# Attention, channel mix and MLP on one core: a pause in score making at block ends, an earlier place for turned loads, a z tile doubled on chip

## The chip, the core and the metric

The kernel runs on one core of a Trainium2 chip. The metric is device time in microseconds. Three runs of the kernel before took 2532.66 to 2536.51 us, median 2535.36 us. The engines are TensorE (PE in the profile; its weight loads are PEld), VectorE (DVE), ScalarE (ACT), GpSimd (POOL) and SyncE (SP), which here only issues transfers.

## What is computed

Three stages follow each other, all in float32. Batch 4, sequence S = 3072, width 256.

```python
scores = (1 / S) * z @ z.T                  # z: 4 x 3072 x 64
x = u * (maximum(scores, 0) ** 2 @ v)       # attention without softmax
xk, xr = mixes of x with x one position back, by mu_k and mu_r
k = maximum(xk @ w_k, 0) ** 2               # 256 -> 1024
x = sigmoid(xr @ w_r) * (k @ w_v)           # 1024 -> 256
out = maximum(x @ w_in, 0) ** 2 @ w_out     # 256 -> 2048 -> 256
```

`u`, `v`, `z` arrive in float32. The weights arrive in float64 and are turned into float32 on the chip by bit operations (`convert`, eight VectorE steps for each piece and two more for a split).

## The kernel before, in words

**Precision.** Every operand of a matmul is split into a high and a low part (`hi` is the operand rounded to the matmul's type, `lo` the rest), and a product takes three matmuls: high by high, high by low of the other side, low by high.

**Tiling of the attention.** Scores are symmetric, so the kernel makes them transposed: a chunk is 128 key positions by a block of T = 512 query positions. A batch has NB = 6 blocks, a block NJ = 24 chunks in NG = 6 groups of G = 4; four batches give 24 blocks and 576 steps. Step s of the main loop (L519) takes chunk s: `attend` (L394) multiplies the chunk with the matching rows of v and adds to two accumulators `d` = 0, 1, each in two halves of 64 rows which two matmuls fill side by side. In a step with j = s mod 24 the order on TensorE differs at a block's ends: steps 0 and 22 do the accumulator 0 alone, steps 1 and 23 catch up on accumulator 1. So step 0 has three pairs of matmuls, steps 1 and 23 nine, step 22 three, and the others six. Within step 0 and 1, all three terms of an accumulator follow each other, the low part of the chunk last.

**Making a chunk.** `scores(s)` (L357) makes a chunk in one of two ways. For a group g at or right of the block's diagonal (g >= ib, ib being the block's number in its batch) TensorE computes two chunks at once into score banks (L371, four banks), ScalarE applies ReLU (L354) and squares (L375), ScalarE or VectorE casts the high part (L380 or L378), VectorE turns the chunk for later use (`turn`, L332, when g > ib) and subtracts the low part (L385). For g < ib the chunk was already computed in its transposed form: it was turned, stored to memory, and is loaded again by `load_turned_scores` (L341) in four quarters q into one of three buffers `mixed`; then it takes only a cast (L363) and a subtraction (L364). The subtraction of a chunk is not issued with it: `finish` (L387) holds it back and issues it when the next chunk is made. In the last block of a batch, the diagonal group comes first.

**Lead.** Chunks are made ahead of their use. The loop at L537 makes chunks up to s + 4 at first, and up to s + 7 later: the lead is 4 up to step 71, 5 up to 95, 6 up to 119 and 7 from step 120. Chunk tiles (`ahi`, `alo`) have eight buffers.

**End of a block.** `gate` (L406) copies the accumulators out. For d = 0, ScalarE copies both halves (L410 `x` and L413 `rest`); for d = 1 it copies one, and VectorE adds the other (L417). Then VectorE adds the halves of d = 0 (L415), multiplies both by the turned u (L424, twice), and SP stores them (L426). The accumulators have one buffer each, so the next block's first matmul waits for L413.

**Order of the work.** The scheduler is off (`manual_schedule`): each engine runs its instructions in the order in which the program issues them, and SP issues transfers in that order as well. The list `todo` holds what a step issues before its own matmuls, in the order of registration (`at_step`): z, v, u loads and their preparation, the weight conversions, and the quarters of turned loads. z tiles are loaded with two copies of the 64 rows (four transfers of 32 partitions each), transposed by VectorE (L267), cast by ScalarE (L274) and subtracted by VectorE (L276). `load_v` (L278) and `prep_v` (L290) do the same for v, through three buffers `raw` that the weight pieces use too.

The two later stages (`channel_mix`, `mlp`) take the rest of the time; the change does not touch them.

Of the kernel before, what the change touches and what calls it, by code (L numbers as in the profile page):

```python
# [7 lines left out]
F32 = mybir.dt.float32  # L8
# [3 lines left out]
ALU = mybir.AluOpType  # L12
# [3 lines left out]
P = 128  # L16
Q = 32
T = 512
# [3 lines left out]
def tile_relu2_attention__rwkv_channel_mix__relu2_mlp(  # L22
# [18 lines left out]
    nc = tc.nc  # L41
# [200 lines left out]
    def attention():  # L242
        with ExitStack() as st:
# [11 lines left out]
                engine.dma_start(out=t[p:p + Q].rearrange("q (k r) -> q k r", r=Q),  # L255
                                 in_=src.rearrange("(q k) r -> q k r" if g in apart else "(k q) r -> q k r", q=Q))

            def load_z(b, g, engines=(nc.sync,) * R):
                z_raw[b, g] = t = io.tile([P, T], F32, tag="zn", name="zn")
                for k, e in enumerate(engines):  # L260
                    d = k * Q % DQ
                    load_turned(t, k * Q, z[b, g * T:(g + 1) * T, d:d + Q], g, e)

            def prep_z(b, g, stage):
                if stage == 0:
                    zT[b, g] = io.tile([P, T], F32, tag="zT", name="zT", bufs=1)
                    nc.vector.transpose(zT[b, g], z_raw.pop((b, g)))  # L267
                    return
                t = zT[b, g]
                if stage == 1:  # L270
                    if g % 2 == 0:
                        zz[b] = zp.tile([P, G, T], F32R, tag="zz", name="zz", bufs=NG // 2)
                    zhi[b, g], zlo[b, g] = (zz[b][:, i, :] for i in (g % 2 * 2, g % 2 * 2 + 1))
# [83 lines left out]
            def scores(s):  # L357
                n, b, ib, g, c = chunk(s)
                if g < ib:
                    a = ready[n, g][:, :, c].rearrange("y p c k -> y c p k")  # L360
                    hi, lo = at[s] = parts(*pools["hidden"])
                    hi_v, lo_v = (t.rearrange("y (c p k) -> y c p k", c=G, k=Q) for t in (hi, lo))
                    nc.scalar.copy(hi_v, a)  # L363
                    finish(lambda: nc.vector.tensor_tensor(out=lo_v, in0=a, in1=hi_v, op=ALU.subtract))  # L364
                    return
                ps = ()
                if c % 2 == 0:
                    ps = [ps_s.tile([P, T], F32, tag="w", name="sps") for _ in HALVES]
                    for k in range(3):
                        for i, rows in enumerate(HALVES):  # L370
                            nc.tensor.matmul(ps[i], lhsT=(zlo, zhi, zhi)[k][b, g][rows, (c + i) * P:(c + i + 1) * P],  # L371
                                             rhs=(zhi, zlo, zhi)[k][b, ib][rows], start=k == 0, stop=k == 2)
                    rel[s] = relu(ps[0])
                a = rel.pop(s)
                nc.scalar.activation(out=a, in_=a, func=AF.Square)  # L375
                hi, lo = at[s] = parts(*pools["hidden"])
                if (g == ib and ib < 3) or (ib < 2 and c == 3) or (ib == 0 and c == 1 and g % 2):
                    nc.vector.tensor_copy(hi, a)  # L378
                else:
                    nc.scalar.copy(hi, a)  # L380
# [53 lines left out]
                todo.setdefault(s, []).append((f, a))  # L434

            n_steps = NBLK * NJ
            for b in range(1, B):
                end = b * NB * NJ
                for g in range(NG):
                    s = end + NJ * (g // 2 - 3) + 6 + 9 * (g % 2)  # L440
                    at_step(s, load_z, b, g)
                    for k in range(3):
                        at_step(s + 7 + 2 * k, prep_z, b, g, k)
                    s = end - NJ + G * ((g + 1) % NG) + 5
                    at_step(s - 8, load_v, b, g)
                    for h in range(2):
                        for lo in range(2):
                            at_step(s + 2 * h + lo, prep_v, b, g, h, lo)
# [4 lines left out]
            for g in range(1, NG):  # L453
                if g > 1:
                    at_step(max(-FIRST, G * g - 15), load_z, 0, g)
                at_step(max(-FIRST, G * g - 12), load_v, 0, g)
                for k in range(3 if g > 1 else 0):
                    at_step(max(1 - FIRST, G * g - 11) + k, prep_z, 0, g, k)
                for h in range(2):
                    for lo in range(2):  # L460
                        at_step(G * g - 5 + 2 * h + lo, prep_v, 0, g, h, lo)
# [3 lines left out]
                    at_step(s + 2 + 9 * d, load_u, n, d)  # L465
                    at_step(s + 10 + 9 * d, prep_u, n, d)

            freed, taken, EARLY = [], 0, 30
            for n in range(NBLK - 1):
                b, ib = divmod(n, NB)  # L470
                for g in range(ib):
                    need, stored = n * NJ + (g + ib // (NB - 1)) * G - LEAD, (b * NB + g) * NJ + ib * G + G - 1 - FIRST
                    s = max(need - EARLY, stored + 1, freed[-3] if len(freed) > 2 else 0, taken)
                    d = max(1, min(3, (need - 3 - s) // 4))
                    for q in range(R):
                        at_step(s + q * d, load_turned_scores, n, g, q)
                    taken = s + 4 * d
                    assert taken <= need - 2
                    freed.append(need + G + 1)
            for g in range(NB - 1):  # L480
                for q in range(R):
                    at_step((NBLK - 1) * NJ + G * g - (15 if g < 2 else 10) + q, load_turned_scores, NBLK - 1, g, q)
            conversions = []
            for w, sb in ((w_k, wk), (w_v, wv), (w_r, wr)):
                for src, cs, fs in pieces(w.bitcast(U32), 2):
# [4 lines left out]
                                lambda: nc.vector.tensor_tensor(out=lo, in0=t, in1=hi, op=ALU.subtract)]  # L490
                    conversions.append((src, keep, 2))
            later = LEAD - FIRST
            free = [t for t in range(NJ, n_steps - NJ) if chunk(t + later)[3] < chunk(t + later)[2] < NB - 1]
            total = sum(8 + rests for _, _, rests in conversions)
            k0 = 0
            for i, (src, done, rests) in enumerate(conversions):
                steps = [free[(k0 + k) * len(free) // total] for k in range(8 + rests)]
                k0 += len(steps)
# [3 lines left out]
            assert total <= len(free)  # L502

            s = n_steps - NJ
            for n in range(2):
                at_step(s - 6 + 12 * n, load_x, n)
# [5 lines left out]
            for wh, m in enumerate((mu_k, mu_r)):  # L512
                nc.sync.dma_start(out=mu[:, wh, :], in_=m.rearrange("(c p) -> p c", p=P))
            for g in range(2):
                for k in range(3):
                    prep_z(0, g, k)
            nc.vector.tensor_scalar(out=om, in0=mu, scalar1=-1.0, scalar2=1.0, op0=ALU.mult, op1=ALU.add)
            made = 0
            for s in range(-FIRST, n_steps + 1):  # L519
                for f, a in todo.pop(s, ()):  # L520
                    f(*a)
                if made == n_steps:
                    finish()
                j = s % NJ if 0 <= s < n_steps else None
                if j in (1, NJ - 1):
                    attend(s, 0, range(3))
                    if j > 1:
                        gate(s // NJ, 0)
                    attend(s - 1, 1, range(3))
# [404 lines left out]
```

## Time and profile before

| | us |
|---|---|
| median of three runs | 2535.36 |
| the profiled execution | 2534.24 |
| its span, first to last instruction | 2532.4 |
| TensorE busy | 2491.6 (98%) |
| VectorE busy | 1967.3 (78%) |
| ScalarE busy | 1725.6 (68%) |
| mean granted clock of TensorE | 0.995 |

Matmuls are pipelined, so a busy TensorE may still run below its peak: at half the clock it is busy as well. The clock has two levels, 1.2 and 2.4 GHz, and the granted clock of a stretch is given as a share of the higher one. The attention fills the time up to about 955 us; there TensorE's chain shows L403 (attend) and L371 (scores). Idle time of an engine that is not on the chain costs nothing by itself.

### The profile page before, as it was taken

How to read it: one execution, taken by the hardware profiler on the slowest of the kernel's cores; microseconds unless marked ns; L12 is line 12 of the kernel's file. 1: busy time of each engine (PE TensorE's matmuls, PEld its weight loads, DVE VectorE, ACT ScalarE, POOL GpSimd, SP SyncE). 2: the span in 40 equal slices, each digit the busy share in tenths (PEclk: the TensorE clock that was granted, in tenths of full speed). 3: DMA queues.
4: the chain of work that ended last, by engine and by line, in shares of the span. 5: the costliest groups of instructions: out<-in, count | busy, mean ns of one | idle time of the engine just before them, and what ended most of it. 6: DMA issues, size and time to landing. Idle time of an engine off the chain costs nothing.

```text
span 2532.4 us, 39521 instructions
## 1 busy us (share of the span) xinstructions
PE 2491.6 (98%) x14832; PEld 2047.4 (81%) x14832; DVE 1967.3 (78%) x3318; ACT 1725.6 (68%) x3015; POOL 0.2 (0%) x4
## 2 busy tenths in 40 slices
PE   7999999999999999999999999999999999999998
PEld 6877788788778878888888888788888888888887
DVE  7786977787777776888888777877777777777776
ACT  7877987788778765555655566666666666666665
POOL 0000000000000000000000000000000000000000
PEclk9999999999999999999999999999999999999999
DMA  8687677676876861222212112100110011100100
GB/s 208 161 207 180 176 199 180 183 206 161 210 191 171 196 159 55 79 84 67 88 59 87 61 48 67 31 20 17 34 34 17 18 34 34 26 25 18 34 17 17
DMA packets 322096, 244.31 MB, mean 96 GB/s; under 512 B 213104, under 2 KB 231536, under 8 KB 321904
## 3 DMA queue, kind: packets, MB, share of 16 engines
q1 hardware_dynamic: 319792, 241.39, 36.2%
q8 instruction: 116, 1.90, 0.3%
q10 hardware_dynamic: 2112, 0.39, 0.1%
q14 instruction: 76, 0.62, 0.1%
HBM read 136.86 MB, written 104.86 MB: 95 GB/s over the span
## 4 chain that ended last, share of the span: by engine, by line
PE 87%; ACT 5%; DVE 3%; DMA 2%; issue 1%; SPq 1%; DVEq 0%; ACTq 0%
PE v L403 25%; PE ups L722 16%; PE ups L208 13%; PE v L738 6%; PE v L739 6%; PE v L740 6%; PE sps L371 4%; PE v L230 3%; PE v L231 3%; PE v L234 3%; ACT a L375 1%; ACT a L354 1%; DMA mixed<-turned 1%; SPq L255 1%; ACT s L762 0%
## 5 line engine op out<-in xcount | busy, mean ns | idle before, releaser
L403 PE MATMUL v<-ahi,vhl 64*128 64x512 f32 x4608 | 646.1, 391 | 14.3 <-ACT rest L413 14.3
L403 PEld LDWEIGHTS v<-ahi,vhl 64*128 64x128 f32 x4608 | 440.2, 186 | 113.2 <-ACT rest L413 20.2
L759 ACT ACTIVATE s<-s 128x512 f32<-128x512 f32 x288 | 181.2, 629 | 333.5 <-DVE s L754 333.4
L403 PE MATMUL v<-alo,vhl 64*128 64x512 f32 x2304 | 381.0, 390 | 7.0 <-DVE alo L385 5.9
L722 PE MATMUL ups<-d,win 128*128 128x512 f32 x1152 | 323.6, 389 | 0.0
L738 PE MATMUL v<-hhi,wout 128*128 128x512 f32 x768 | 299.3, 390 | 0.9 <-ACT hhi L767 0.6
L740 PE MATMUL v<-hlo,wout 128*128 128x512 f32 x768 | 299.2, 390 | 0.5 <-DVE hlo L773 0.5
L739 PE MATMUL v<-hhi,wout 128*128 128x512 f32 x768 | 298.8, 389 | 0.0
L208 PE MATMUL ups<-mixed,wk 128*128 128x512 f32 x1152 | 291.8, 389 | 0.0
L773 DVE TENSOR_TENSOR hlo<-s,hhi 128x512 fp32r<-128x512 f32 x384 | 264.5, 689 | 21.8 <-ACT hhi L767 8.9
L160 ACT ACTIVATE a<-ups 128x512 f32<-128x512 f32 x192 | 114.9, 599 | 238.4 <-PE ups L208 231.6
L403 PEld LDWEIGHTS v<-alo,vhl 64*128 64x128 f32 x2304 | 222.3, 186 | 56.4 <-DVE alo L385 10.3
L208 PEld LDWEIGHTS ups<-mixed,wk 128*128 128x128 f32 x1152 | 216.2, 188 | 44.9
L722 PEld LDWEIGHTS ups<-d,win 128*128 128x128 f32 x1152 | 216.3, 188 | 44.8
L722 PE MATMUL ups<-b,win 128*128 128x512 f32 x864 | 242.9, 389 | 0.0
L385 DVE TENSOR_TENSOR alo<-a,ahi 128x512 fp32r<-128x512 f32 x336 | 220.6, 660 | 26.5 <-ACT ahi L380 24.3
L762 ACT ACTIVATE s<-s 128x512 f32<-128x512 f32 x384 | 231.2, 627 | 6.1
L332 DVE STREAM_TRANSPOSE turn<-a 128x512 f32<-128x512 f32 x240 | 169.4, 706 | 71.6 <-ACT a L375 71.6
L354 ACT ACTIVATE a<-sps 128x512 f32<-128x512 f32 x336 | 198.6, 591 | 31.4 <-PE sps L371 30.9
L375 ACT ACTIVATE a<-a 128x512 f32<-128x512 f32 x336 | 212.5, 633 | 10.1
L363 ACT CAST ahi<-mixed 128x512 fp32r<-128x512 f32 x220 | 126.5, 619 | 104.6 <-PE v L403 42.5
L722 PEld LDWEIGHTS ups<-b,win 128*128 128x128 f32 x864 | 162.0, 188 | 34.2 <-DVE sv L754 0.8
(103 smaller groups left out, 3672.1 us busy)
## 6 DMA issues: line engine op xcount, KB each, us to landing
mixed<-turned SPq DMA_DIRECT2D x220, 256.0 KB, 4.6
turned<-turn SPq DMA_DIRECT2D x36, 1024.0 KB, 5.2
turned<-turn SPq DMA_DIRECT2D x96, 256.0 KB, 4.0
u<-in_u_dram SPq DMA_DIRECT2D x192, 64.0 KB, 3.8
x2d<-xo SPq DMA_DIRECT2D x48, 256.0 KB, 2.2
x<-x2d SPq DMA_DIRECT2D x12, 1024.0 KB, 4.8
out_dram<-y SPq DMA_DIRECT2D x94, 128.0 KB, 2.8
x<-xT SPq DMA_DIRECT2D x20, 513.0 KB, 4.0
```

The lines of the kernel that those rows point to most:

```text
L208: nc.tensor.matmul(ps, lhsT=lhs(h, c, f), rhs=rhs[:, m, c, :], start=k == 0, stop=k == 3 * ND - 1)
L354: nc.scalar.activation(out=a, in_=ps, func=AF.Relu, scale=1.0 / S)
L375: nc.scalar.activation(out=a, in_=a, func=AF.Square)
L385: finish(lambda: nc.vector.tensor_tensor(out=lo, in0=a, in1=hi, op=ALU.subtract))
L403: nc.tensor.matmul(acc[n, d][i], lhsT=vt[rows, k % 2, c, ds_], rhs=at[s][k // 2][rows], start=first and k == 0, stop=last and k == 2)
L722: nc.tensor.matmul(ps, lhsT=win[q][:, h, r, w], rhs=x(y), start=first and m == 0, stop=m == 2, skip_group_check=not first)
L738: nc.tensor.matmul(acc[p, b][d], lhsT=w[:, 0, c, ds_], rhs=hi, start=first, stop=False)
L739: nc.tensor.matmul(acc[p, b][d], lhsT=w[:, 1, c, ds_], rhs=hi, start=False, stop=False)
L740: nc.tensor.matmul(acc[p, b][d], lhsT=w[:, 0, c, ds_], rhs=lo, start=False, stop=last)
L759: nc.scalar.activation(out=tmp[g, c], in_=banks[g, 0] if c == "11" else tmp[g, c], func=AF.Relu, scale=HS)
L762: nc.scalar.activation(out=tmp[g, c], in_=tmp[g, c], func=AF.Square)
L773: nc.vector.tensor_tensor(out=lo, in0=tmp.pop((g, c)), in1=hi, op=ALU.subtract)
```

## The change

The loop makes no chunk in steps j = 21 and 22 of a block; what is missing is made in step 23, after the gates. The turned loads are registered first, so that in a step they are issued ahead of z, u and v, and the release of their buffers is planned one step earlier (`need + G` for `need + G + 1`). From batch 1 on, a z tile is loaded once (64 rows) and transposed in 64 partitions, and a transfer from on-chip memory to on-chip memory makes the second copy; the cast follows four steps after the transposition instead of two. The third and later z tiles of batch 0 are prepared two steps later. The weight conversions are spread over the batches, so that none reaches from one batch into the next. The loads of mu and `om` move from the start to steps 48 and 72. The condition of the cast's engine becomes wider: VectorE casts all chunks of the diagonal group and every fourth chunk of a group.

```diff
-            def load_z(b, g, engines=(nc.sync,) * R):
+            def load_z(b, g, engines=None):
                 z_raw[b, g] = t = io.tile([P, T], F32, tag="zn", name="zn")
-                for k, e in enumerate(engines):
+                for k, e in enumerate(engines or (nc.sync,) * (R if b == 0 else R // 2)):
                     d = k * Q % DQ
                     load_turned(t, k * Q, z[b, g * T:(g + 1) * T, d:d + Q], g, e)
 
             def prep_z(b, g, stage):
                 if stage == 0:
-                    zT[b, g] = io.tile([P, T], F32, tag="zT", name="zT", bufs=1)
-                    nc.vector.transpose(zT[b, g], z_raw.pop((b, g)))
+                    rows = slice(0, P if b == 0 else DQ)
+                    zT[b, g] = t = io.tile([P, T], F32, tag="zT", name="zT", bufs=1)
+                    nc.vector.transpose(t[rows], z_raw.pop((b, g))[rows])
+                    if b > 0:
+                        nc.sync.dma_start(out=t[DQ:P], in_=t[rows])
                     return
...
-                if (g == ib and ib < 3) or (ib < 2 and c == 3) or (ib == 0 and c == 1 and g % 2):
+                if g == ib or c == 3 or (ib == 0 and c == 1 and g % 2):
                     nc.vector.tensor_copy(hi, a)
...
+            freed, taken, EARLY = [], 0, 30
+            for n in range(NBLK - 1):
+                b, ib = divmod(n, NB)
+                for g in range(ib):
+                    need, stored = n * NJ + (g + ib // (NB - 1)) * G - LEAD, (b * NB + g) * NJ + ib * G + G - 1 - FIRST
+                    s = max(need - EARLY, stored + 1, freed[-3] if len(freed) > 2 else 0, taken)
+                    d = min(3, (need - 3 - s) // 4) or 0.5
+                    for q in range(R):
+                        at_step(s + int(q * d), load_turned_scores, n, g, q)
+                    taken = s + int(4 * d)
+                    assert taken <= need - 2
+                    freed.append(need + G)
...
             for b in range(1, B):
...
                     at_step(s, load_z, b, g)
                     for k in range(3):
-                        at_step(s + 7 + 2 * k, prep_z, b, g, k)
+                        at_step(s + (7, 11, 13)[k], prep_z, b, g, k)
...
                 for k in range(3 if g > 1 else 0):
-                    at_step(max(1 - FIRST, G * g - 11) + k, prep_z, 0, g, k)
+                    at_step(G * g - 9 + k, prep_z, 0, g, k)
...
-            freed, taken, EARLY = [], 0, 30
-            for n in range(NBLK - 1):
...
-                    d = max(1, min(3, (need - 3 - s) // 4))
-                    for q in range(R):
-                        at_step(s + q * d, load_turned_scores, n, g, q)
-                    taken = s + 4 * d
-                    assert taken <= need - 2
-                    freed.append(need + G + 1)
...
-            free = [t for t in range(NJ, n_steps - NJ) if chunk(t + later)[3] < chunk(t + later)[2] < NB - 1]
-            total = sum(8 + rests for _, _, rests in conversions)
-            k0 = 0
             for i, (src, done, rests) in enumerate(conversions):
+                b = i * B // len(conversions)
+                mine = [k for k in range(len(conversions)) if k * B // len(conversions) == b]
+                free = [t for t in range(b * NB * NJ, (b + 1) * NB * NJ - NJ)
+                        if chunk(t + later)[3] < chunk(t + later)[2] < NB - 1]
+                k0, total = (i - mine[0]) * (8 + rests), len(mine) * (8 + rests)
                 steps = [free[(k0 + k) * len(free) // total] for k in range(8 + rests)]
...
+            at_step(2 * NJ, load_mu)
+            at_step(3 * NJ, make_om)
...
-                while made < min(n_steps, s + 1 + min(LEAD, FIRST + max(0, s - 2 * NJ) // NJ)):
+                ahead = 0 if j in (NJ - 3, NJ - 2) else min(LEAD, FIRST + max(0, s - 2 * NJ) // NJ)
+                while made < min(n_steps, s + 1 + ahead):
                     scores(made)
                     made += 1
```

## Rows read from the trace of the kernel before

**Rows 1.** The page: busy time, share and instructions of each engine.
```profile
PE 2491.6 (98%) x14832; PEld 2047.4 (81%) x14832; DVE 1967.3 (78%) x3318; ACT 1725.6 (68%) x3015; POOL 0.2 (0%) x4
```

**Rows 2.** Waits of TensorE, whole span: total us, times, longest us.
```profile
PE v L403 <- ACT rest L413: 14.3, 7, 3.7
...
PE sps L371 <- ACT a L354: 4.5, 5, 2.0
```

**Rows 3.** Table by stretches: length, busy us by engine, granted clock, DMA share, GB/s.
```profile
218.60:260.40 41.80, 39.08 (x312) 31.37 (x312) 30.43 (x50) 25.91 (x48) 0.00 (x0) 0.93 0.68 184
260.40:300.00 39.60, 39.58 (x348) 32.66 (x350) 35.81 (x64) 35.17 (x62) 0.00 (x0) 1.00 0.77 214
...
493.30:534.00 40.70, 40.69 (x344) 34.55 (x346) 35.99 (x64) 35.14 (x61) 0.00 (x0) 0.96 0.76 208
...
687.00:729.00 42.00, 39.41 (x312) 31.25 (x312) 29.46 (x49) 25.16 (x48) 0.00 (x0) 0.92 0.71 181
```

**Rows 4.** Timeline of TensorE at three block ends: start, us, [idle before, releaser].
```profile
218.59 1.22 PE L403 MATMUL v<-ahi,vhl 64*128 64x512 f32 x4 [3.65 <-ACT rest L413]
...
260.42 0.73 PE L403 MATMUL v<-ahi,vhl 64*128 64x512 f32 x4 [2.70 <-ACT rest L413]
...
493.31 0.73 PE L403 MATMUL v<-ahi,vhl 64*128 64x512 f32 x4 [2.70 <-ACT rest L413]
```

**Rows 5.** The chain that ended last, one piece: start us, us, what.
```profile
72.06 2.72 PE v L403 x24
```

**Rows 6.** Timeline of SP and ScalarE, 239 to 248 us.
```profile
239.70 3.52 SPq L285 DMA_DIRECT2D raw<-in_v_dram  x4
243.27 0.59 SPq L348 DMA_DIRECT2D mixed<-turned  x1
...
246.53 1.14 ACT L363 CAST ahi<-mixed 128x512 fp32r<-128x512 f32 x2 [6.17 <-PE v L403]
```

**Rows 7.** Groups by line: the two casts; count, busy us, mean ns, idle before.
```profile
L380 ACT CAST ahi<-a 128x512 fp32r<-128x512 f32 x240 | 149.3, 622 | 7.7
...
L378 DVE CAST ahi<-a 128x512 fp32r<-128x512 f32 x96 | 40.3, 420 | 24.7 <-ACT a L375 24.1
```

**Rows 8.** Timeline of TensorE and VectorE at the first four block ends.
```profile
61.70 0.62 PE L403 MATMUL v<-ahi,vhl 64*128 64x512 f32 x4
64.38 0.68 DVE L364 TENSOR_TENSOR alo<-mixed,ahi 128x512 fp32r<-128x512 f32 x1
...
100.46 0.70 PE L403 MATMUL v<-ahi,vhl 64*128 64x512 f32 x4
103.82 1.29 DVE L364 TENSOR_TENSOR alo<-mixed,ahi 128x512 fp32r<-128x512 f32 x2
...
139.21 0.68 PE L403 MATMUL v<-ahi,vhl 64*128 64x512 f32 x4
143.34 0.67 DVE L364 TENSOR_TENSOR alo<-mixed,ahi 128x512 fp32r<-128x512 f32 x1
144.06 0.73 PE L403 MATMUL v<-alo,vhl 64*128 64x512 f32 x4 [0.72 <-DVE alo L364]
...
177.29 0.70 PE L403 MATMUL v<-ahi,vhl 64*128 64x512 f32 x4
181.48 0.67 DVE L364 TENSOR_TENSOR alo<-mixed,ahi 128x512 fp32r<-128x512 f32 x1
```

**Rows 9.** Timeline of the first block: waits of VectorE, TensorE and ScalarE.
```profile
13.40 0.71 DVE L267 STREAM_TRANSPOSE zT<-zn 128x512 f32<-128x512 f32 x1 [1.88 <-DMA zn<-in_z_dram]
15.07 0.79 PE L403 MATMUL v<-alo,vhl 64*128 64x512 f32 x2 [3.00 <-DVE alo L385]
...
38.34 0.62 ACT L274 CAST zz<-zT 128x512 fp32r<-128x512 f32 x1 [1.97 <-DVE zT L267]
```

**Rows 10.** Transfers by line: queue, count, KB each, median us from issue to landing.
```profile
mixed<-turned SPq DMA_DIRECT2D x220, 256.0 KB, 4.6
...
zn<-in_z_dram SPq DMA_DIRECT2D x94, 64.0 KB, 3.5
```

More of the change, by code (lines that the diff above doesn't have):

```diff
@@ L265, in prep_z @@
                 if stage == 0:
-                    zT[b, g] = io.tile([P, T], F32, tag="zT", name="zT", bufs=1)
-                    nc.vector.transpose(zT[b, g], z_raw.pop((b, g)))
+                    rows = slice(0, P if b == 0 else DQ)
[3 more added lines that the diff above has]
+                        nc.sync.dma_start(out=t[DQ:P], in_=t[rows])
                     return
-                t = zT[b, g]
+                t, k = zT[b, g], g % 2 * 2
                 if stage == 1:
@@ L272, in prep_z @@
                         zz[b] = zp.tile([P, G, T], F32R, tag="zz", name="zz", bufs=NG // 2)
-                    zhi[b, g], zlo[b, g] = (zz[b][:, i, :] for i in (g % 2 * 2, g % 2 * 2 + 1))
+                    zhi[b, g], zlo[b, g] = (zz[b][:, k + i, :] for i in range(2))
                     nc.scalar.copy(zhi[b, g], t)
@@ L436, in attention @@
             n_steps = NBLK * NJ
+            freed, taken, EARLY = [], 0, 30
[10 more added lines that the diff above has]
+                    freed.append(need + G)
+            for g in range(NB - 1):
+                for q in range(R):
+                    at_step((NBLK - 1) * NJ + G * g - (15 if g < 2 else 10) + q, load_turned_scores, NBLK - 1, g, q)
             for b in range(1, B):
@@ L466, in attention @@
                     at_step(s + 10 + 9 * d, prep_u, n, d)
-            freed, taken, EARLY = [], 0, 30
-            for n in range(NBLK - 1):
[L470 to L473, printed above, removed]
-                    d = max(1, min(3, (need - 3 - s) // 4))
-                    for q in range(R):
-                        at_step(s + q * d, load_turned_scores, n, g, q)
-                    taken = s + 4 * d
-                    assert taken <= need - 2
-                    freed.append(need + G + 1)
-            for g in range(NB - 1):
-                for q in range(R):
-                    at_step((NBLK - 1) * NJ + G * g - (15 if g < 2 else 10) + q, load_turned_scores, NBLK - 1, g, q)
             conversions = []
@@ L492, in attention @@
             later = LEAD - FIRST
-            free = [t for t in range(NJ, n_steps - NJ) if chunk(t + later)[3] < chunk(t + later)[2] < NB - 1]
-            total = sum(8 + rests for _, _, rests in conversions)
-            k0 = 0
             for i, (src, done, rests) in enumerate(conversions):
+                b = i * B // len(conversions)
[3 more added lines that the diff above has]
+                k0, total = (i - mine[0]) * (8 + rests), len(mine) * (8 + rests)
                 steps = [free[(k0 + k) * len(free) // total] for k in range(8 + rests)]
-                k0 += len(steps)
                 at_step(steps[0] - 10, load_raw, ("w", i), src, src.shape[1], src.shape[2])
@@ L501, in attention, with load_mu, make_om @@
                     at_step(t, f)
-            assert total <= len(free)
+                assert total <= len(free)
+            def load_mu():
+                for wh, m in enumerate((mu_k, mu_r)):
+                    nc.sync.dma_start(out=mu[:, wh, :], in_=m.rearrange("(c p) -> p c", p=P))
+            def make_om():
+                nc.vector.tensor_scalar(out=om, in0=mu, scalar1=-1.0, scalar2=1.0, op0=ALU.mult, op1=ALU.add)
+            at_step(2 * NJ, load_mu)
+            at_step(3 * NJ, make_om)
             s = n_steps - NJ
@@ L511, in attention @@
             load_v(0, 0)
-            for wh, m in enumerate((mu_k, mu_r)):
-                nc.sync.dma_start(out=mu[:, wh, :], in_=m.rearrange("(c p) -> p c", p=P))
             for g in range(2):
@@ L516, in attention @@
                     prep_z(0, g, k)
-            nc.vector.tensor_scalar(out=om, in0=mu, scalar1=-1.0, scalar2=1.0, op0=ALU.mult, op1=ALU.add)
             made = 0
```

## The prediction, made before the changed kernel ran

> **What bounds the kernel now.** I read the page's busy times first. TensorE is busy for 98% of the span [rows 1], so a change of order can only take away TensorE's pauses and its slow stretches. Next I read the waits of TensorE itself, over the whole span: 14.3 us in seven waits for the copy `rest` of L413, and 4.5 us in five waits of the score matmuls for a ReLU of L354 [rows 2]. Then the table by stretches, for the granted clock: three stretches in which the attention passes from one block to the next stand at 0.93, 0.92 and 0.96, where the block between two of them has 1.00 [rows 3]. A share below 1 is time at 1.2 GHz instead of 2.4, and each microsecond there does half a microsecond of work. So 41.8 us at 0.93 lose 0.07 x 41.8 = 2.9 us, 42.0 at 0.92 lose 3.4, 40.7 at 0.96 lose 1.6; together 7.9. Last, the timeline around the seven waits: they stand at the ends of blocks, the longest being 3.65 us, and two of 2.70 shown beside it [rows 4]. All lie in the attention; the two MLP stages are not touched.
>
> One unit is needed: 24 matmuls of 64 rows, two of which run side by side, take 2.72 us [rows 5]. So two chunk steps are 2.72, one is 1.36, and a term of one accumulator pair (two matmuls) is 0.227 us.
>
> **What takes time at the end of a block.** TensorE may only start the next block when ScalarE has copied the accumulators out (L410, L413). ScalarE has chunk work queued ahead of those copies. One source of lateness is a late turned load: SP held the load of the last quarter behind four v loads until 243.27, and ScalarE, idle for 6.17 us, began the cast at 246.53 [rows 6] (the row names TensorE, which had long been done; the load is what came last). The block's end then waited 2.70 us, until 260.42 [rows 4]. The pattern stands three times, once at the end of each of the first three batches.
>
> **The change, part by part.**
>
> *Turned scores first, no chunk in steps 21 and 22.* In steps 21 and 22 ScalarE's queue now holds no chunk ahead of the copies, and in step 23 three chunks come after them. The quarters are issued a step earlier and ahead of the v and z loads of their step. Of the 14.3 us I let all go except 1.5 at the boundary from block 4 to 5 (worked out below) and 1 at the start of each later batch: there every chunk needs ReLU and square, and the three chunks that were put off stand in front of the ReLU which frees the score banks, so TensorE waits at L371 instead. Bounds of that remainder: 0, and the 2.70 seen there. 14.3 - 1.5 - 3 = 9.8. The score waits came from the late loads: 4.5 less 0.5 at the start of the program gives 4.0. The slow stretches followed these waits; all 7.9 go. Sum so far 21.7.
>
> *More casts on VectorE.* 72 casts (18 per batch: in blocks 2 to 5 all four chunks on the diagonal from block 3 on, and the fourth chunk of each group to its right) move from 622 ns on ScalarE to 420 ns on VectorE [rows 7]. That is 45 us off ScalarE, which is late at block ends, and 30 us onto VectorE. I give it no term of its own: it is one more reason for the 9.8. Its cover is VectorE's idle time in these stretches (30.4 busy of 41.8 [rows 3]).
>
> *The price: a low part that is now late.* The low part of a chunk (L364 or L385) is issued with the chunk after it. With nothing made in steps 21 and 22, the low part of the chunk made in step 20 comes in step 23, behind the four gate operations L417, L415 and twice L424. How late that is, rows tell: at the end of block 2 TensorE has done the block at 139.21, and the first low part after the gates runs from 143.34 to 144.01. TensorE already waits for it in the kernel before, 0.72 us, until 144.06 [rows 8]; there it is the third chunk of the block. How early TensorE needs it depends on the lead. It is 7 chunks from step 120 on, and then the late one is the fourth of the new block, wanted after 0.68 + 2.04 + 1.36 + 0.91 = 4.99 us against 4.80 at which it is there: no wait. But the lead is 4 up to step 71, 5 in step 95 and 6 in step 119. With 4, the late low part belongs to the first chunk of the block, wanted 0.45 us after the block begins. I set the end of the first low part after the gates against the need [rows 8]:
> - block 0 to 1: 65.06 (64.38 + 0.68) against 61.70 + 0.45: 2.9 us
> - block 1 to 2: 104.46 (half of two in 1.29, from 103.82) against 100.46 + 0.45: 3.6
> - block 2 to 3: 144.01 against 139.21 + 0.45: 4.4, less the 0.7 that already stood there
> - block 3 to 4 (lead 5, one step of 0.68 more): 182.15 against 177.29 + 0.68 + 0.45: 3.7
> - block 4 to 5 (lead 6): there at 4.80 plus a cast of 0.42, wanted at 0.68 + 2.04 + 0.91 = 3.63: 1.5, as taken above.
>
> The first four add 13.9 us of waits. Queued behind the waiting matmul is all of TensorE's work, and nothing later gives the time back.
>
> Waits of this length may also halve the clock. Rows go both ways: after 3.65 us the stretch stands at 0.93 (2.9 us lost); after 2.70 at 260.42 it stays at 1.00; after the other 2.70, at 0.96 (1.6 lost) [rows 3, 4]. Bounds: none of four falls, 0; all fall, 4 x 2.9 = 11.6. I take 6, the two longer ones falling. The Trainium skill, TensorE: Matmul & The Clock Gate, section "What's actually happening", says that the slow clock is the default state and that activity releases it. By that rule each long wait would be paid again behind it, and the sum would be near the upper bound; the stretch at 1.00 after 2.70 us does not agree with it for every wait.
>
> *Third z tile later.* At the start VectorE stands at the transpose of the third z tile (waiting for its load, 1.88 us, until 13.40), and the first low part stands behind it; TensorE waits 3.00 us, until 15.07 [rows 9]. Moved two steps on, the first low part needs only its own cast: I take 2.5 of the 3.0 (bounds 0 and 3.0). The same for the sixth tile: ScalarE waits 1.97 us for its transpose, until 38.34 [rows 9], in a block in which TensorE waits for ScalarE's chunks: 2.0 (bounds 0 and 2.0). Sum 4.5. The two loads of `mu` and the small VectorE operation on them leave the start too; I cost that at nothing.
>
> *z doubled on chip.* In batches 1 to 3 a z tile takes two loads of 64 KB instead of four, and one copy of 128 KB from the transposed half. Loads of z land after 3.5 us, the turned quarters of 256 KB after 4.6 [rows 10]; the copy lies between or near these, and ScalarE asks for it four steps later, about 5.4 us. At nothing, since chunks lie ready ahead. What it costs when that cover is gone is the third rival.
>
> *Conversions inside a batch.* The same 90 small operations in other steps, in stretches where VectorE has room [rows 3]; at nothing, bound by one such operation of 0.7 us on either side per batch.
>
> **Sum.** 21.7 + 4.5 - 13.9 - 6 = 6.3 us gained. The profiled execution took 2534.24 us, 1.84 more than its span; by the change 2527.9. The median of the runs shown is 1.12 above it, so 2529.0.
>
> **The rivals.**
> 1. *The early low parts are not late* (something issues them ahead of the gates, or TensorE has other work there). Then the 13.9 and the 6 fall away: 26.2 gained, 2509. Against it: the wait at 144.06 is this very queue.
> 2. *They are late, but the clock holds*: 12.3 gained, 2523. For it speaks the 1.00 behind 260.42.
> 3. *Slower: SP is held, and ScalarE behind it.* A turned load in step 21 of some blocks (3 to 4, 9 to 10, 15 to 16, 21 to 22) takes over a buffer whose last low part now waits behind the gates, to 4.8 us after the block's end. Behind it in SP's queue stands the new z copy of step 22. Issued some 1.2 us later and landed after 4.6 [rows 10], it lets ScalarE cast z and the next chunk by 4.8 + 1.2 + 4.6 + 2 x 0.62 = 11.8; TensorE wants that chunk (the tenth of the block) at 0.68 + 2.04 + 7 x 1.36 = 12.2. So it decides from a landing of 5.0 us on. With 8 us TensorE would wait 3.4 in three blocks, and at 2.9 of slow clock each that is 19 lost: 12.6 slower, 2548. Against it: 4.6 is the usual landing. The Trainium skill, DMA: Bandwidth & Descriptors, section "Anatomy of one DMA", says that any semaphore wait happens on the issuing sequencer before dispatch; that is the hold described here.
> 4. *No change*: all four early waits drop the clock (11.6 instead of 6): 0.7 gained, 2534.7. This is what the clock rule cited above would make of it.
>
> **How the numbers follow.** Forecast 0.42, rival 1 0.12, rival 2 0.18, rival 3 0.12, rival 4 0.16. About 0.2%, 5 us, is what a measurement of this kernel can tell from no change: faster is below 2530.3, slower above 2540.4. The forecast's own range is 2523 to 2535, from the clock's bounds; 0.7 of it counts as faster. Faster: 0.42 x 0.7 + 0.12 + 0.18 = 0.60; slower: rival 3, 0.12; within: 0.28. The range 2512 to 2538 leaves out the far end of rivals 1 and 3.
>
> **What would show it.** In the profile after: no wait of TensorE for L413 over 1 us; new waits of TensorE for L364 or L385 of 3 to 4.5 us at the first four block ends, near 60, 100, 139 and 178 us, and none at those of later batches; granted clock under 1 in two of these four stretches and 1.00 where it was 0.92 to 0.96; the first wait for a low part at the start gone. The forecast is wrong if the early block ends show no such wait (2509), or if TensorE waits in blocks 4, 10, 16 and 22 for ScalarE while ScalarE waits for z.

## The result: 0.56% slower, and where the profile after shows it

The changed kernel took 2548.9 us (median of six runs, 2543.57 to 2551.91), before on the same chip 2534.69: a ratio of 1.0056, with a 95% interval of 1.0043 to 1.0069. The forecast was 2529 us, 6.3 gained; 14.2 were lost. The profiled execution of the changed kernel, called after below, took 2547.61 us, its span 2545.8. The lines named here have moved by up to three: the copy `rest` is now L416, a turned chunk's low part L367, a fresh chunk's L388, the attention's matmul L406, the ReLU L357, the z cast L277; the new z copy is L270.

First the page's busy times of after, against [rows 1]: VectorE has 72 instructions of the casts more, ScalarE 72 fewer and 40.5 us less work, as the change says. TensorE's share stays at 98%.

```profile
PE 2495.3 (98%) x14832; PEld 2061.4 (81%) x14832; DVE 1988.6 (78%) x3390; ACT 1685.1 (66%) x2943; POOL 0.2 (0%) x4
```

Next the waits of TensorE in after (total us, times, longest us).

```profile
PE v L406 <- DVE alo L367: 18.9, 6, 4.1
PE v L406 <- DVE alo L388: 6.8, 7, 3.9
...
PE v L406 <- ACT rest L416: 5.5, 4, 2.0
PE sps L374 <- ACT a L357: 2.5, 3, 0.8
```

Against [rows 2] the waits for `rest` went from 14.3 us to 5.5 and those of the score matmuls from 4.5 to 2.5. In their place stand 18.9 us for the low parts of turned chunks. Four of these six are the late low parts of the prediction. The timeline of after at the third of them (start, us, what, and in brackets the idle time before with its releaser) shows the queue:

```profile
151.57 0.69 DVE L420 TENSOR_TENSOR x<-v,x 128x512 f32<-128x512 f32 x1 [1.84 <-ACT x L413]
152.18 0.68 DVE L418 TENSOR_TENSOR x<-rest,x 128x512 f32<-128x512 f32 x1
152.89 1.04 DVE L427 TENSOR_TENSOR rest<-x,uT 128x512 f32<-128x512 f32 x1
153.97 1.04 DVE L427 TENSOR_TENSOR x<-x,uT 128x512 f32<-128x512 f32 x1
154.85 1.88 DVE L367 TENSOR_TENSOR alo<-mixed,ahi 128x512 fp32r<-128x512 f32 x3
155.58 0.61 PE L406 MATMUL v<-alo,vhl 64*128 64x512 f32 x2 [4.14 <-DVE alo L367]
```

The low part starts behind the four gate operations, and TensorE starts when it is done. The other three end at 67.38, 111.38 and 198.46, after 2.81, 3.40 and 3.43 us; a fifth, for a fresh chunk's low part, at 239.43 after 1.11. [rows 8] are the first places before.

The other two of the six were not in the forecast. The longer one stands at the last block of the first batch, where TensorE had its best chance to gain. Timeline of after, SP, ScalarE, VectorE and TensorE:

```profile
258.74 4.32 SPq L255 DMA_DIRECT2D u<-in_u_dram  x4
259.16 0.70 DVE L268 STREAM_TRANSPOSE zT<-zn 64x512 f32<-64x512 f32 x1 [3.49 <-DMA zn<-in_z_dram]
263.24 2.80 SPq L288 DMA_DIRECT2D raw<-in_v_dram  x4
266.14 0.54 SPq L270 DMA_DIRECT2D zT<-zT  x1
269.20 0.62 ACT L277 CAST zz<-zT 128x512 fp32r<-128x512 f32 x1 [4.10 <-DMA zT<-zT]
271.01 0.43 DVE L381 CAST ahi<-a 128x512 fp32r<-128x512 f32 x1 [6.40 <-ACT a L378]
271.35 0.69 DVE L367 TENSOR_TENSOR alo<-mixed,ahi 128x512 fp32r<-128x512 f32 x1
272.09 0.79 PE L406 MATMUL v<-alo,vhl 64*128 64x512 f32 x2 [3.54 <-DVE alo L367]
```

VectorE had the half of z transposed by 259.86. SP was issuing four u loads and then four v loads, and came to the copy at 266.14. ScalarE, free from 265.10, stood until it had landed, and behind ScalarE stood VectorE (6.40) and then TensorE (3.54). The waits of ScalarE in after say how often: ten times, 40.0 us; the kernel before has no such copy to wait for. Eight of the eighteen copies were issued 3.0 to 7.6 us after their transposition had ended, and 37.2 of the 40.0 us stand behind these eight.

```profile
ACT zz L277 <- DMA zT<-zT: 40.0, 10, 6.9
```

Last the table by stretches of after (length, busy us of the five engines, granted clock, DMA share, GB/s): blocks 1 to 5, and the last blocks of the second and third batch.

```profile
64.10:108.10 44.00, 41.08 (x348) 36.09 (x344) 33.00 (x57) 34.31 (x60) 0.00 (x0) 0.96 0.59 160
108.10:151.50 43.40, 40.06 (x336) 36.64 (x336) 31.39 (x54) 30.59 (x54) 0.00 (x0) 0.96 0.63 159
151.50:194.40 42.90, 38.82 (x328) 36.55 (x329) 32.80 (x57) 27.59 (x50) 0.00 (x0) 0.96 0.70 162
194.40:235.00 40.60, 37.17 (x328) 30.22 (x326) 31.39 (x55) 25.80 (x48) 0.00 (x0) 1.00 0.74 169
235.00:278.40 43.40, 38.59 (x320) 30.35 (x316) 29.50 (x50) 25.18 (x46) 0.00 (x0) 0.96 0.70 175
...
470.50:510.40 39.90, 36.67 (x320) 29.36 (x316) 28.60 (x47) 23.97 (x45) 0.00 (x0) 1.00 0.75 192
702.50:741.00 38.50, 36.86 (x320) 29.39 (x316) 28.61 (x48) 24.41 (x46) 0.00 (x0) 1.00 0.75 195
```

The slow clock behind three of the early waits and behind the one at 272.09 costs 0.04 x 43.4 = 1.7 us each; it stands right behind the waits (granted clock 0.61 from 67.4 to 71.4 and 0.74 from 272.0 to 278.4). The later batches hold 1.00 (also from 510.4 to 551.0), where before had 0.96 and 0.92 [rows 3].

### The profile page after: what moved, and what is told of

The parts are those of the page before. It is cut to its first block, busy times and chain, and to the rows that moved or that the text cites. A ratio compares the mean times of both kernels' runs of the same rounds, so it can differ in the third digit from the quotient of the medians.

```text
span 2545.8 us, 39407 instructions
## 1 busy us (share of the span) xinstructions
PE 2495.3 (98%) x14832; PEld 2061.4 (81%) x14832; DVE 1988.6 (78%) x3390; ACT 1685.1 (66%) x2943; POOL 0.2 (0%) x4
## 4 chain that ended last, share of the span: by engine, by line
PE 87%; DVE 4%; ACT 3%; DMA 2%; SPq 2%; issue 1%; DVEq 0%; ACTq 0%
PE v L406 25%; PE ups L733 16%; PE ups L208 13%; PE v L749 6%; PE v L750 6%; PE v L751 6%; PE sps L374 4%; PE v L234 3%; PE v L230 3%; PE v L231 3%; DMA mixed<-turned 1%; ACT a L357 1%; ACT a L378 1%; SPq L255 1%; SPq L351 1%
## 5 line engine op out<-in xcount | busy, mean ns | idle before, releaser
L406 PE MATMUL v<-ahi,vhl 64*128 64x512 f32 x4608 | 675.4, 391 | 6.8 <-ACT rest L416 5.5
L406 PEld LDWEIGHTS v<-ahi,vhl 64*128 64x128 f32 x4608 | 472.7, 186 | 97.4 <-ACT rest L416 10.7
L406 PE MATMUL v<-alo,vhl 64*128 64x512 f32 x2304 | 414.0, 392 | 26.0 <-DVE alo L367 18.9
L406 PEld LDWEIGHTS v<-alo,vhl 64*128 64x128 f32 x2304 | 250.4, 186 | 74.1 <-DVE alo L367 21.9
L357 ACT ACTIVATE a<-sps 128x512 f32<-128x512 f32 x336 | 198.6, 591 | 40.3 <-PE sps L374 36.8
L388 DVE TENSOR_TENSOR alo<-a,ahi 128x512 fp32r<-128x512 f32 x336 | 221.0, 661 | 0.0
L335 DVE STREAM_TRANSPOSE turn<-a 128x512 f32<-128x512 f32 x240 | 169.4, 706 | 40.5 <-ACT a L378 35.6
L765 DVE TENSOR_TENSOR s<-ups,su 128x512 f32<-128x512 f32 x192 | 131.2, 683 | 58.8 <-PE ups L733 58.8
```

The source lines that it names most:

```text
L357: nc.scalar.activation(out=a, in_=ps, func=AF.Relu, scale=1.0 / S)
L406: nc.tensor.matmul(acc[n, d][i], lhsT=vt[rows, k % 2, c, ds_], rhs=at[s][k // 2][rows], start=first and k == 0, stop=last and k == 2)
```

## The experiments

A run's cost or gain below is the difference of two ratios to before, times 2535 us; the two intervals together leave it open by some 4 to 5 us. Two times from each profiled execution, one execution each, help to place it: the start of VectorE's add for d = 1 at the end of block 4 (L417 before, L420 after), and the time from there to the start of TensorE's last matmul.

| kernel | ratio (95%) | end of block 4 | from there to the last matmul |
|---|---|---|---|
| before | 1 | 219.1 | 2306.1 |
| the change | 1.0056 (1.0043 to 1.0069) | 235.0 | 2303.6 |
| e1: pause from block 5 on | 0.9974 (0.9964 to 0.9983) | 218.2 | 2303.6 |
| e2: z as before | 1.0011 (1.0002 to 1.0020) | 238.2 | 2291.8 |
| e3: conversions as before | 1.0057 (1.0042 to 1.0072) | 235.2 | 2302.8 |
| e4: before, with the pause alone | 1.0055 (1.0038 to 1.0071) | 232.5 | 2306.2 |
| e5: held low parts issued ahead | 1.0011 (1.0002 to 1.0020) | 229.0 | 2302.5 |
| e6: e1, e2 and e3 together | 0.9927 (0.9915 to 0.9939) | 217.3 | 2291.3 |
| e9: e6, third z tile as before | 0.9915 (0.9901 to 0.9928) | 214.7 | 2291.4 |
| e10: e6 without any pause | 0.9932 (0.9919 to 0.9944) | 217.3 | 2294.3 |
| e11: e6, casts as before | 0.9958 (0.9946 to 0.9971) | 217.9 | 2298.5 |
| e12: e6, turned loads as before | 0.9954 (0.9941 to 0.9966) | 213.2 | 2302.4 |
| e13: the change, z copy on GpSimd | 1.0011 (1.0002 to 1.0020) | 237.3 | 2295.3 |
| e14: e9, z doubled, copy on GpSimd | 0.9913 (0.9900 to 0.9927) | 215.3 | 2293.6 |

**e1: no pause in the first five blocks.**

```diff
-ahead = 0 if j in (NJ - 3, NJ - 2) else min(LEAD, ...)
+ahead = 0 if j in (NJ - 3, NJ - 2) and s >= 5 * NJ else min(LEAD, ...)
```

> The changed kernel, with the pause in steps 21 and 22 only from step 120 on, where the lead is 7 chunks. Theory: at the block ends near 67, 111, 155 and 198 us TensorE waits 2.97, 3.56, 4.30 and 3.60 us for a low part that is issued behind the gates, with some 5 us of half clock after three of them, and 1.3 at 239; all of that goes, some 19 us: 2530 us (2526 to 2534). Rival: what is slow is any pause, by the three chunks that pile up in step 23 and the score banks they hold; then the early waits shrink, but come back elsewhere, and the time stays above 2540.

Measured 2530.15 us: 0.0082 x 2535 = 20.8 us come back, and the waits at the first block ends are gone. Waits of TensorE in e1:

```profile
PE v L406 <- DVE alo L367: 7.4, 4, 2.5
...
PE v L406 <- ACT rest L416: 3.9, 2, 2.3
```

So the early pause costs 20.8. The prediction had 13.9 + 1.5 of waits and 6 of slow clock, 21.4.

**e2 and e3: z loaded as before; conversions placed as before.** In e2 the two loads become four and L270 goes; in e3 `free`, `total` and `k0` are those of before.

```diff
-(nc.sync,) * (R if b == 0 else R // 2)
+(nc.sync,) * R
...
-rows = slice(0, P if b == 0 else DQ)
+rows = slice(0, P)
...
-if b > 0:
-    nc.sync.dma_start(out=t[DQ:P], in_=t[rows])
...
-at_step(s + (7, 11, 13)[k], prep_z, b, g, k)
+at_step(s + 7 + 2 * k, prep_z, b, g, k)
```

> The changed kernel, with the z tiles of batches 1 to 3 loaded four times 64 KB and cast two steps after their transposition, as before. Theory: at the ends of batches ScalarE stands at the cast of z until the on-chip copy has landed (40.0 us in ten waits), and TensorE waits for what is queued behind it (near 272, 504, 509, 735, 740 us, with score-bank waits after it); without the copy ScalarE's waits for it are gone and 8 to 14 us come back: 2538 us (2534 to 2543). Rival: ScalarE is late there because the v loads now stand behind the turned loads (12.0 us of waits for raw v); then TensorE's waits near 272 and 509 stay, and less than 4 us come back.

> The changed kernel, with the weight conversions spread over all batches as before, so that the first weight load is issued in step 14 and not in step 11. Theory: that load of 512 KB now stands in front of the store of the third turned group (46.35 us); the staging tile is not free until 53.3, VectorE stands 3.7 us at the turn, TensorE 3.94 until 54.63, and half clock follows: 7 us come back, 2542 us (2539 to 2545). Rival: the store is late because SP was held by the u loads (5.90 us for four); then the wait near 54 us stays and the time is within 2 us of the changed kernel.

e2: 2538.57 us, 11.4 come back, as expected. In its profile 11.8 us are won behind block 4 (2303.6 to 2291.8) and 3.2 lost ahead of it. Its waits of TensorE lack the last block's ones in the first two batches; in the third one of 1.57 us for `rest` stays:

```profile
PE v L404 <- DVE alo L365: 13.8, 4, 4.1
...
PE v L404 <- ACT rest L414: 3.2, 2, 1.6
```

e3: 2550.85 us, a miss: none of the 7 us came back, though the store is early as the theory has it. SP issues it at 43.80, and not behind a weight load at 46.35 (the four u loads also took 4.66 us there and not 5.90), TensorE's wait near 54 us shrinks from 3.94 to 2.23, and block 0 ends 2.5 us earlier (61.64 for 64.11). But the end of block 4 is where it was. In this profile block 4 gives the 2.5 us back: the clock falls behind the fourth early wait, where it stayed at 1.00 in after. That stretch in e3's table (columns as above):

```profile
192.10:235.20 43.10, 39.69 (x328) 34.84 (x326) 31.10 (x54) 25.74 (x47) 0.00 (x0) 0.92 0.71 170
```

**e13: what makes the copy late.** Only its issuing engine changes.

```diff
-nc.sync.dma_start(out=t[DQ:P], in_=t[rows])
+nc.gpsimd.dma_start(out=t[DQ:P], in_=t[rows])
```

> The changed kernel (2548.9, 1.0056 of before) with only the on-chip copy of z issued by GpSimd, which issues nothing else, in place of SP. Theory (the copy is late because SP issues it behind four u loads and four v loads: transposed by 259.86, issued 266.14; and because SP stands at it): about 8 of the 10.3 us that the loads of before gave back in e2 come back here too, 2541 (2538 to 2543), and ScalarE's waits for the copy (40.0 us in ten) shrink to under 15. Rival (the copy itself, or its traffic, takes the time, wherever it is issued): 2546 to 2551, ScalarE's waits stay.

Measured 2539.61 us, 1.0011: the same ratio as with the loads of before in e2, 11.4 us back. Timeline of e13 at the place shown above, GpSimd, VectorE and ScalarE, and then ScalarE's waits:

```profile
260.77 0.70 DVE L268 STREAM_TRANSPOSE zT<-zn 64x512 f32<-64x512 f32 x1 [3.82 <-DMA zn<-in_z_dram]
262.02 0.52 POOL L270 DMA_DIRECT2D zT<-zT  x1 [26.60 <-DVE zT L268]
263.41 1.14 ACT L366 CAST ahi<-mixed 128x512 fp32r<-128x512 f32 x2 [4.53 <-DMA raw<-in_v_dram]
266.55 0.61 ACT L277 CAST zz<-zT 128x512 fp32r<-128x512 f32 x1
```

```profile
ACT zz L277 <- DMA zT<-zT: 6.5, 6, 3.1
```

The copy is issued 0.55 us after the transposition's end and not 6.28, and ScalarE casts z without waiting for it (it stands 4.53 us for a v load ahead of that, which TensorE does not feel); 40.0 us of its waits become 6.5. The copy itself is no faster (median to landing 4.2 us, 3.4 on SP). It was SP's queue. (In after SP also stood at the copy itself for its transposition, 26.6 us in five waits; GpSimd takes this hold off SP as well, and no run parts the two.) The Trainium skill, DMA: Bandwidth & Descriptors, section "Anatomy of one DMA", says that a semaphore wait happens on the issuing sequencer; the trace agrees, GpSimd standing 26.60 us ahead of this copy, with nothing behind it that anyone wants.

**e4: the pause alone, put into the kernel before.**

> The kernel before with the pause in steps 21 and 22 of every block and nothing else of the change. Theory (the low part behind the gates): the four early waits of 2.9 to 4.4 us and one of 1.3 stand at the same block ends, with half clock after two or three of them, some 19 us lost; the waits for the copy at L413 (14.3 us) and the slow stretches behind them mostly go, 12 to 18 us gained: 2538 us (2534 to 2544). Rival (the pause costs only in company of the other parts, by the order on SP): no early waits, and faster than the kernel before by 10 us or more.

A miss of 13 us: 2551.0. The early waits stand as expected, but later boundaries gain nothing (2306.2 against 2306.1). Waits of TensorE in e4:

```profile
PE v L403 <- DVE alo L364: 16.2, 7, 4.1
PE v L403 <- ACT rest L413: 11.9, 6, 3.8
```

Of the 14.3 us for `rest` [rows 2] 11.9 remain. So the pause by itself hardly makes ScalarE early.

**e6: the change without its three suspects; e10: and without the pause; e11, e12: and without the casts, or the order.** e6 is e1, e2 and e3 in one. e10 takes the pause out of e6, e11 puts back the old condition of the casts, e12 the old block of `load_turned_scores` steps, behind v and z. The four expectations stand in the order e6, e10, e11, e12.

> The three reversals together: pause only from step 120 on, z and conversions as before. What is left of the change: the pause with a lead of 7, turned loads first, third z tile later, mu later, more casts on VectorE. Theory: the three prices add up, 19 + 10 + 7 = 36 us off the changed kernel: 2513 us (2507 to 2521), faster than the kernel before by 0.5 to 1.1%. Rival: the prices share one cause (each late chunk lets the next wait vanish), or the gains forecast for the late block ends are not there: 2528 or more.

> The kernel with the three reversals (2517.5 us), without any pause. Theory: the pause at a lead of 7 is what lets TensorE pass the block ends, so waits for the copy at L413 return, 0.7 to 2.7 us at several of the later ends: 2524 us (2520 to 2530). Rival: the casts on VectorE and the order of the turned loads already make ScalarE early enough: within 2 us of 2517.5.

> The kernel of e6 (2517.5, 0.9927 of before) with the casts of the high parts on the engines that had them before. Theory (the gain of e6 over before comes mostly from ScalarE having fewer casts at the block ends): some 10 us go back, 0.9966 of before, about 2528 (2523 to 2533), and TensorE waits again for `rest` at the batch ends, where every chunk needs ReLU, square and cast on ScalarE. Rival (the gain comes from the turned loads going ahead of the v and z loads): within 3 us of e6, 2515 to 2520, no such waits.

> The kernel of e6 (2517.5, 0.9927 of before) with the turned loads issued in the order and at the steps of before, behind the v and z loads. Theory (casts carry most of the gain): 3 to 6 us go back, 2522 (2519 to 2525), with waits at the ends of blocks 4, 10 and 16 (near 218, 452, 687), where SP had the last quarter behind v loads. Rival (the order carries it): 10 us and more go back, 2527 to 2533.

e6: 2517.49 us, 18.5 faster than before. The last column takes the gain behind block 4 apart, 2306.1 to 2291.3. Without the order 11.1 us of it are lost (2302.4), without the casts 7.2 (2298.5), without the pause 3.0 (2294.3). By the ratios of whole runs these are 6.8, 7.9 and 1.3: the first two are told from nothing, but not from each other, and the pause is not told from nothing, though waits for `rest` return with it gone (7.9 us in four, for 3.0 in two in e6). Whether casts outweigh order, as I had it, stays open: of e12's 6.8 us, 11.1 are lost behind block 4 and 4.1 are won ahead of it (213.2 for 217.3), all of them by the end of block 0 (59.87 for 63.98), where e6's wait of 2.93 us near 54 us is not there. Its waits stand elsewhere than expected, in the last block of each batch. Timeline of e12, SP, ScalarE and TensorE:

```profile
235.06 2.50 SPq L286 DMA_DIRECT2D raw<-in_v_dram  x4
237.60 0.59 SPq L349 DMA_DIRECT2D mixed<-turned  x1
242.40 1.14 ACT L364 CAST ahi<-mixed 128x512 fp32r<-128x512 f32 x2 [6.68 <-DMA u<-in_u_dram]
253.32 0.73 PE L404 MATMUL v<-ahi,vhl 64*128 64x512 f32 x4 [1.65 <-ACT rest L414]
```

This is the picture of [rows 6]: a turned quarter behind four v loads, ScalarE idle, the block's end late. (The row names u; what this cast reads is the quarter.) The casts matter one block earlier, at the ends of blocks 4, 10, 16 and 22. Timeline of e11 there; the ReLU, square and cast of the chunks on ScalarE follow each other without a gap from 204.88 until the copies begin at 216.29:

```profile
215.24 0.62 ACT L381 CAST ahi<-a 128x512 fp32r<-128x512 f32 x1
...
216.29 0.58 ACT L411 COPY x<-v 128x512 f32<-128x512 f32 x1
217.40 0.73 PE L404 MATMUL v<-ahi,vhl 64*128 64x512 f32 x4 [1.40 <-ACT rest L414]
```

**e5: the held low part issued ahead of the pause.** The pause stays in every block.

```diff
+if j == NJ - 3:
+    finish()
```

> The changed kernel, in which the low part held back is issued in step 21, so that only what is made in step 23 stands behind the gates. Theory: then the next chunk's low part is the first behind the gates, and TensorE wants it only one step later, so the early waits shrink but stay: 2.2 us at block 0 to 1, 2.9 at 1 to 2, 3.7 at 2 to 3, 1.2 at 3 to 4, next to none at 4 to 5, against 2.97, 3.56, 4.30, 3.60 and 1.27: 5.5 us less, with up to 3 of slow clock: 2542 us (2538 to 2545). Rival: the one low part that is late is all that is wrong with the pause; then all early waits go, and it is 2530.

2540.57 us, 11.4 back, within the range. TensorE's first waits at these places become 2.01, 2.01, 2.75 and 0.77 us, somewhat less than expected: the held low part is early now, the next ones still come after the gates.

**e9: the third z tile as before; e14: the same with z doubled on chip and the copy on GpSimd.**

```diff
-at_step(G * g - 9 + k, prep_z, 0, g, k)
+at_step(max(1 - FIRST, G * g - 11) + k, prep_z, 0, g, k)
```

> The kernel with the three reversals (2517.5 us), in which the z tiles from the third on of batch 0 are prepared as early as in the kernel before. Theory: z and u share two buffers; z held two steps longer delays the u loads on SP, the store of the third turned group behind them, and with it VectorE near 53 us; undone, TensorE's wait of 3.10 us at 54.4 and the slow clock behind it go, and the wait of 3.0 us at 15 returns: the first block ends at 61 to 62 instead of 64.0, 2515 us (2512 to 2518). Rival: the u loads are slow by the traffic alone: the wait at 54 stays, the start loses its 2 to 3 us, 2520.

> The kernel of e9 (2515.4, 0.9915 of before) with z doubled on chip, the copy issued by GpSimd. Theory (with no hold on SP's queue the copy is hidden): within 3 us of e9, 0.9904 to 0.9927 of before, 2512 to 2518. Rival (the copy costs as in the changed kernel): 8 to 10 us above e9, 2523 to 2526.

e9: 2515.37 us; the wait near 54 us is gone and block 0 ends at 61.39 instead of 63.98. But the wait of 3.0 us near 15, which the theory had return, did not: it is 0.99 us, until 13.71. e14: 2514.21 us. The two can't be told apart; they beat before by 0.85 and 0.87%. Waits of TensorE in e9:

```profile
PE v L404 <- DVE alo L386: 4.5, 5, 1.5
PE v L404 <- ACT rest L414: 2.7, 2, 2.3
PE sps L372 <- ACT a L355: 1.9, 6, 0.5
```

## Why the prediction was wrong

Between 6.3 us gained and 14.2 lost lie 20.5. The step that failed is *z doubled on chip*, set at nothing: it cost 11.4. The second is *third z tile later*, set at 4.5 gained: in this kernel it cost some 3.0. The other terms came near their size.

*Turned scores first, casts and pause, slow stretches: 21.7, right in size.* That sum holds the late low part of block 4 to 5, so the gain alone was 23.2; e9, which has these parts and neither the early pause, the copy nor the later z tile, is 0.0085 x 2535 = 21.5 faster than before (some of it won at the start, see the third z tile). The 1 us at the start of each later batch came as 0.79, 0.84 and 0.84. The share was wrong: I gave the pause and the order the 9.8 and the casts no term. The casts carry 7.9 by whole runs, the order 6.8, the pause 1.3, which is not told from nothing. In after itself more than this gain was spent again, as follows.

*The low part that is late: 13.9 + 1.5 and 6 of clock, right.* Forecast were 2.9, 3.6, 3.7 more than before, 3.7 and 1.5; after has 2.81, 3.40, 3.42 more (4.14 less 0.72), 3.43 and 1.11, 14.2 for 15.4. The clock fell behind the first three (0.96 each), 5.2 us for 6. That this total fits is luck: the 6 stood for two falls of 2.9, and there were three of 1.7. Rival 4 had all four fall, and the fourth did not. The Trainium skill, TensorE: Matmul & The Clock Gate, section "What's actually happening", has the slow clock as the default that activity releases; of four waits alike in length three agree, and 1.00 in the stretch with 3.43 us of wait does not. In e4 the same four waits leave other stretches slow (the first at 1.00, the fourth at 0.92):

```profile
63.10:102.90 39.80, 39.13 (x342) 31.88 (x342) 30.02 (x54) 31.56 (x55) 0.00 (x0) 1.00 0.64 175
...
189.20:229.90 40.70, 37.29 (x306) 31.12 (x303) 28.40 (x46) 28.56 (x51) 0.00 (x0) 0.92 0.73 170
```

Which wait pays is not settled by these runs.

*z doubled on chip, "at nothing": the step that failed.* I set the copy's landing (3.5 to 4.6 us) against the 5.4 us until ScalarE asks for it, and left out what the copy stands behind: SP issues in order, and in the last block of a batch eight loads, 4.32 and 2.80 us, come first. 6.28 us passed before the copy was issued, more than the whole cover of 5.4. Price 11.4 us (e2), and the copy on GpSimd gives it back (e13). The waits of TensorE in e2 sum to 9.4 us less than in after, and the slow clock behind 272.09 makes 1.7 more.

Rival 3 had SP held and ScalarE standing at the cast of z, and this came where it said, at blocks 3 to 4, 9 to 10 and 15 to 16. There SP stands at a turned load for the late low part (L367; 4.5, 4.5 and 5.8 us), the copy behind it goes out late, and ScalarE stands 6.87, 5.66 and 6.19 us. The first of these in after, SP and ScalarE (the 7.53 us hold the wait of 4.5):

```profile
192.90 7.53 SPq L351 DMA_DIRECT2D mixed<-turned  x4
200.47 0.51 SPq L270 DMA_DIRECT2D zT<-zT  x1
204.40 0.62 ACT L277 CAST zz<-zT 128x512 fp32r<-128x512 f32 x1 [6.87 <-DMA zT<-zT]
```

But TensorE does not pay there: it has no wait of 0.7 us or more between 198.46 and 239.43. The rival's own sum had that cover (11.8 against 12.2). TensorE pays in the last blocks of the batches, where eight plain loads stand ahead of the copy, and neither the forecast nor a rival had that. So the rival's total (2548) came out by chance; besides, with a landing of 8 us its own numbers make TensorE wait 3.0 us and not 3.4. The row for plain loads that hold SP up was there [rows 6].

*Third z tile later: +4.5 forecast, a loss.* The start gained about what was said: for the wait of 3.00 us until 15.07 [rows 9] one of 0.63 until 14.04. At the sixth tile ScalarE still waits 1.43 us, until 39.34, for 1.97. But that gain is not shown to come from this step: e9, which has the third tile as before, waits only 0.99 there, and its granted clock from 10 to 20 us is 1.00 where before has 0.66. What e9 shares with after at the start is that the two loads of mu are gone from SP's queue (0.51 and 0.47 us ahead of the third tile's loads), which the prediction cost at nothing; and e4, with the start of before, waits 1.94 until 14.26, so part of it changes from run to run. No run parts these. The loss, then: the third tile's transposition is at 13.90 for 13.40, the fourth at 21.98 for 20.24, the fifth at 29.76 for 28.32, and what follows on SP is later: in after the third group's turned chunks are stored at 46.35 for 43.79. Timeline of after in block 0:

```profile
38.68 5.90 SPq L255 DMA_DIRECT2D u<-in_u_dram  x4
44.68 1.57 SPq L94 DMA_DIRECT2D raw<-in_moe_w_k_dram  x1
46.35 0.41 SPq L342 DMA_DIRECT2D turned<-turn  x1
53.29 0.71 DVE L335 STREAM_TRANSPOSE turn<-a 128x512 f32<-128x512 f32 x1 [3.71 <-DMA turned<-turn]
54.63 0.80 PE L406 MATMUL v<-alo,vhl 64*128 64x512 f32 x2 [3.94 <-DVE alo L388]
```

VectorE waits for the store to free the tile `turn`, and TensorE for VectorE; from 54.6 to 61.0 the granted clock is 0.56. With the third tile as before (e9) the u loads take 3.81 us of SP's time, the store is at 43.31, and this wait is gone: 0.0012 x 2535 = 3.0 us, less than these intervals can tell from nothing; the end of block 0, 2.6 us earlier, speaks for it. The later tile costs this only together with the turned loads going first: e12 has the later tile and the old order, its u loads take 3.02 us, and block 0 ends at 59.87. In all nine kernels with both, these four loads hold SP for 4.66 to 6.45 us, in the other five for 3.02 to 3.86. Why, was not tried.

*Conversions at nothing:* right (e3).

With these the sum closes: -21.5 of gains, +20.8 early pause, +11.4 copy, +3.0 third tile make 13.7 us slower; measured were 14.2.

## What to carry to other kernels

When a transfer is moved or added, cost it from the moment its queue gets to it: add up what the issuing engine issues ahead of it in that step and the steps before, and only then the landing. When a pause in production shifts work behind a boundary, ask at each boundary how far ahead the consumer is at that moment; here the same pause cost 20.8 us at a lead of 4 to 6, and at a lead of 7 it gave 1.3 by whole runs, which is not told from nothing. Undoing one part at a time in the changed kernel parted the losses from the gains and left a version 0.85% faster than before.

## What the runs showed of the hardware that was not expected

A copy of 128 KB within the chip's memory takes about as long to land as a load of 64 KB from outside: medians of 3.4 and 3.7 us in after. Four loads of u held SP's sequencer for anything from 1.93 us (at 22.71 in after) to 5.90 (at 38.68; one of the four alone took 3.79, and the profile has no wait of SP in it), so the time to issue a transfer is not a constant of its shape. The DMA share in these two stretches was 0.37 and 1.10; but in e9 the same loads took 3.81 us at 1.06, so the share alone does not say it. The first and the fourth early wait of TensorE (2.81 and 3.43 us in after) are followed by 0.96 and 1.00 there, and by 1.00 and 0.92 in e4.
